# Seven block products for eight in the second output product of a two-layer gated network, with TensorE's order written out

## The chip, the cores and the metric

The program runs on one core of one Trainium2 chip. Its time is the device time of one execution, in microseconds (us). The kernel before takes 1388.17 us in the median of three runs (1387.19 to 1388.61).

## The reference

An attention with 32 memory slots for 8 batches of 8 heads (576 positions, head size 64) gives 4608 rows of 512. Two feed-forward blocks follow:

```python
def _moe_ref(x, w1, w2, w3, w_out) -> np.ndarray:      # d_ff 768
    h = np.maximum(np.maximum(x @ w1, x @ w2), x @ w3)
    return (h @ w_out).astype(np.float32)

def _moe2_ref(x, w_gate, w_val, w_out) -> np.ndarray:  # d_ff 1536
    gate = 1.0 / (1.0 + np.exp(-(x @ w_gate)))
    val = x @ w_val
    return (gate * val @ w_out).astype(np.float32)
```

All is float32. The change is in the last line, `gate * val @ w_out`: 4608 x 1536 by 1536 x 512.

## The kernel before

**Numbers.** An operand is split into a high part (a cast to a narrower float, by ScalarE: ACT) and the low rest (a subtraction, by GpSimd or VectorE: POOL or DVE); `w_split` does it. A product of two split operands is three matmuls, low by high, high by low, high by high (`PASSES`), added up in PSUM.

**Phase A** (to about 559 us) makes the attention and the first feed-forward block for pairs of batches, and writes its result to DRAM as `x2s`. While it ends, the first operands of phase B are loaded and split.

**Phase B** computes the second feed-forward block. The tokens are cut into five superchunks `sc` of 2 x 512, 2 x 512, 2 x 512, 2 x 384 and 2 x 384 tokens (`SUPER`, the 512 or 384 is `half`), the 1536 columns of gate and value into six pairs `j` of 128-wide slices (j and j + 6). One (sc, j) is called a chunk here; there are 18 with half 512 and 12 with half 384. In a chunk, x @ w is a 2 x 2 block product with seven products for eight (`ORDER` is 1, 6, 2, 7, 5, 4, 3), for gate (v = 0) and value (v = 1): `up(sc, j, pr, v)` is six matmuls of 128 x half. Sums between products are taken as PSUM is read. A finished block (c, h), c the half of the tokens and h the slice, goes through `block_done`: gate to a sigmoid, value times gate to a tile `gf`, and `gf` is split into `gg`. Block (0, 0) is finished by product 2, (1, 1) by 5, (1, 0) by 4 and (0, 1) by 3.

`down(sc, j, c, m)` multiplies 128 tokens of the two `gg` of half c by the two 128 x 512 slices of w_out: six matmuls of 128 x 512 into one PSUM bank `po` (two buffers), which are then copied (j = 0, ACT) or added (DVE, L777) to `acc`. A chunk has 8 (half 512) or 6 of them; they are traced between the `up` of the next chunk, and after j = 5 the rows are stored. The split parts of w_gate and w_val (`tb`) and of w_out (`wo`) are made in superchunk 0 (`t_make`, `wo_make`) and loaded from DRAM in the others (`t_load`, `wo_load`). The operand x of the next superchunk is loaded, summed and split (`x_load`, `x_sums`, `x_split`: tiles `xf`, `xa`) during the last chunks of the one before.

**What sets the order.** A scheduler lays the traced instructions out, engine by engine, in the order of its own timeline; each engine then works through its list in that order and waits on semaphores at the head of it. In phase B the scheduler sets TensorE's order as well.

Of the kernel before, what the change touches and what calls it, by code (L numbers as in the profile page):

```python
# [18 lines left out]
def attn_moe_kernel(  # L19
# [31 lines left out]

    def dma(o, i):
        ins = sync.dma_start(o, i)
# [334 lines left out]
    def x2_step(p, u, d):  # L388
        ps = bank()
        n = 0  # L390
        for j in range(J):
            for x, y in PASSES:
                pe.matmul(  # L393
                    ps[:, :U],
                    lhsT=wo1_t[:, x, (d * J + j) * 128:(d * J + j) * 128 + 128],
                    rhs=H[u, j][:, y],
                    start=(n == 0), stop=(n == 3 * J - 1),
                )
# [88 lines left out]
    def wo_load(sc, j):  # L487
        for h in range(2):
            t = WO[sc, j, h] = q4_tile("wo2")
            dma(f32(t), wos[j + h * NJ])  # L490
# [220 lines left out]

    def block_done(sc, j, v, c, h, ps, other):
# [18 lines left out]
        act.copy(t[:, 0, :half], gf)  # L731
        sub(pool, t[:, 1, :half], gf, f32(t[:, 0, :half]))

    def up(sc, j, pr, v):
# [12 lines left out]
        elif pr in (6, 7):  # L747
            u = E["u", pr, v] = small(f"u{pr}", 2)[:, :half]
            vec.tensor_tensor(out=u, in0=ps[:, :half], in1=E["p1", v], op=ALU.add)  # L749
# [9 lines left out]
    def down(sc, j, c, m):  # L759
        t0, half = SUPER[sc]  # L760
        ps = psB.tile([128, DM], F32, tag="po", name="po", bufs=2)
        n = 0
        for h in range(2):
            for x, y in PASSES:
                pe.matmul(  # L765
                    ps,
                    lhsT=GG[sc, j, c, h][:, x, 128 * m:128 * m + 128],
                    rhs=WO[sc, j, h][:, y],
                    start=(n == 0), stop=(n == 5),
                )  # L770
                n += 1
        if j == 0:
            t = ACC[sc, c, m] = b2.tile([128, DM], F32, tag="acc", name="acc", bufs=8)
            act.copy(t, ps)
        else:
            t = ACC[sc, c, m]
            vec.tensor_tensor(out=t, in0=ps, in1=t, op=ALU.add)  # L777
# [102 lines left out]
```

## Time and profile before

| what | us |
|---|---|
| median of three runs | 1388.17 |
| profiled execution: its time, its span | 1387.49, 1385.4 |
| busy in the span: TensorE matmul (PE) | 1337.5 |
| DVE, ACT, POOL | 863.1, 576.3, 514.6 |
| one chunk of half 512, of half 384, in the middle of a superchunk | 30.03, 22.70 |

A name such as `gg<-gf` is the tile written and the tiles read. PEld is the load of the stationary operand of a matmul, which overlaps the matmuls. L73 is the subtraction in a helper, whoever calls it.

### The profile page before, as it was taken

What the parts mean: (1) busy time and instruction counts of PE and PEld (TensorE: products, weight loads), DVE (VectorE), ACT (ScalarE), POOL (GpSimd) and SP (SyncE); (2) the same over time, 40 slices, a digit from 0 to 9 for tenths busy, and PEclk for the clock granted to TensorE, in tenths of its full rate; (3) what the DMA queues carried; (4) which work ended last, traced back from release to release, by engine and by line L of the source; (5) the groups of instructions that cost most, each with busy time, mean ns of one, the idle gap of its engine ahead of it and who ended that gap; (6) DMA issues with size and microseconds to landing.
All of it is one profiled execution on the core that took longest, in us unless ns stands there. A gap on an engine that the chain in (4) does not pass through costs nothing.

```text
span 1385.4 us, 22143 instructions
## 1 busy us (share of the span) xinstructions
PE 1337.5 (97%) x7864; PEld 1183.9 (85%) x7864; DVE 863.1 (62%) x1533; ACT 576.3 (42%) x1220; POOL 514.6 (37%) x454
## 2 busy tenths in 40 slices
PE   6688999999999999999999999999999999999998
PEld 3578899999999989788888888888888899999997
DVE  5999759966975895566765344453445444554454
ACT  5687546645654664453343321233222322233221
POOL 2775422422331227553586111461112712161111
PEclk9899999999999999999999999999999999999999
DMA  9588757776757745965556544465454666566651
GB/s 314 178 273 304 265 171 262 238 236 225 235 165 261 240 131 170 336 243 198 198 198 228 183 166 153 167 205 190 159 178 167 210 228 222 198 227 237 211 202 72
DMA packets 112269, 292.43 MB, mean 211 GB/s; under 512 B 12576, under 2 KB 28960, under 8 KB 112160
## 3 DMA queue, kind: packets, MB, share of 16 engines
q1 hardware_dynamic: 112160, 291.03, 61.9%
q8 instruction: 62, 1.02, 0.3%
q14 instruction: 47, 0.39, 0.1%
HBM read 224.92 MB, written 66.06 MB: 210 GB/s over the span
## 4 chain that ended last, share of the span: by engine, by line
PE 79%; DVE 10%; DMA 4%; issue 2%; ACT 2%; POOL 1%; SPq 1%; DVEq 0%; ACTq 0%; POOLq 0%
PE po L765 21%; PE px L698 15%; PE pv L698 10%; PE pz L698 10%; PE ps L393 9%; PE ps L370 8%; DVE g L73 2%; PE ps L343 2%; PE ps L209 1%; PE ps L246 1%; DVE ca L129 1%; DVE ca L128 1%; DMA raw<-wb_dram 1%; DVE hm L382 1%; DVE hm L381 1%
## 5 line engine op out<-in xcount | busy, mean ns | idle before, releaser
L765 PE MATMUL po<-wo,gg 128*128 128x512 f32 x1296 | 327.8, 392 | 1.0 <-POOL gg L73 1.0
L73 POOL TENSOR_TENSOR gg<-gf,gg 128x512 fp32r<-128x512 f32 (+1 forms) x120 | 143.4, 1195 | 469.1 <-ACT gg L731 426.3
L765 PEld LDWEIGHTS po<-wo,gg 128*128 128x128 f32 x1296 | 242.4, 188 | 49.5 <-POOL gg L73 1.3
L370 PE MATMUL ps<-attn,g 128*128 128x288 f32 x1728 | 258.7, 302 | 21.0 <-DVE g L73 11.0
L370 PEld LDWEIGHTS ps<-attn,g 128*128 128x128 f32 x1728 | 244.7, 193 | 31.8 <-DVE hm L381 8.7
L698 PE MATMUL px<-xa,tb 128*128 128x512 f32 (+1 forms) x1080 | 244.1, 368 | 1.6 <-DVE gf L729 1.1
L777 DVE TENSOR_TENSOR acc<-po,acc 128x512 f32<-128x512 f32 x180 | 124.3, 691 | 176.0 <-PE po L765 175.8
L698 PEld LDWEIGHTS px<-xa,tb 128*128 128x128 f32 x1080 | 198.0, 188 | 30.4 <-DVE gf L729 1.6
L698 PE MATMUL pz<-xa,tb 128*128 128x512 f32 (+1 forms) x720 | 169.5, 368 | 1.8 <-DVE u L749 1.8
L698 PE MATMUL pv<-xa,tb 128*128 128x512 f32 (+1 forms) x720 | 170.4, 369 | 0.0
L73 POOL TENSOR_TENSOR h<-hm,h 128x288 fp32r<-128x288 f32 x96 | 82.7, 864 | 211.8 <-DVE h L70 111.3
L393 PE MATMUL ps<-h,wo 128*128 128x288 f32 x1152 | 158.5, 296 | 0.0
L393 PEld LDWEIGHTS ps<-h,wo 128*128 128x128 f32 x1152 | 154.3, 188 | 2.8 <-issue 2.6
L698 PEld LDWEIGHTS pz<-xa,tb 128*128 128x128 f32 x720 | 132.2, 188 | 20.9 <-issue 2.2
L698 PEld LDWEIGHTS pv<-xa,tb 128*128 128x128 f32 x720 | 132.8, 189 | 18.1
L731 ACT CAST gg<-gf 128x512 fp32r<-128x512 f32 (+1 forms) x120 | 69.4, 578 | 176.3 <-DVE gf L727 130.5
L749 DVE TENSOR_TENSOR u<-pz,p 128x512 f32<-128x512 f32 (+1 forms) x120 | 76.2, 635 | 97.9 <-PE pz L698 93.4
L73 DVE TENSOR_TENSOR g<-ps,g 64x384 fp32r<-64x384 f32 x180 | 99.4, 552 | 31.8 <-ACT g L357 28.8
L721 ACT ACTIVATE sg<-sg 128x512 f32<-128x512 f32 (+1 forms) x90 | 53.1, 590 | 145.4 <-DVE sg L719 145.1
L357 ACT CAST g<-ps 64x384 fp32r<-64x384 f32 x192 | 90.7, 473 | 36.4 <-DVE g L73 22.4
L73 POOL TENSOR_TENSOR xa<-xf,xa 128x512 fp32r<-128x512 f32 (+1 forms) x64 | 78.8, 1252 | 21.6 <-ACT xa L134 21.6
L727 DVE TENSOR_TENSOR gf<-gf,sg 128x512 f32<-128x512 f32 (+1 forms) x90 | 70.9, 788 | 10.9 <-ACT sg L721 1.3
(92 smaller groups left out, 1394.4 us busy)
## 6 DMA issues: line engine op xcount, KB each, us to landing
tb<-tbs SPq DMA_DIRECT2D x168, 512.0 KB, 3.8
wx<-wxs SPq DMA_DIRECT2D x72, 384.0 KB, 3.9
wo<-wos SPq DMA_DIRECT2D x48, 512.0 KB, 5.4
tbs<-tb SPq DMA_DIRECT2D x42, 512.0 KB, 2.9
raw<-wb_dram SPq DMA_DIRECT2D x48, 384.0 KB, 3.5
kv<-kvm_dram SPq DMA_DIRECT2D x48, 256.0 KB, 5.3
raw<-wx_dram SPq DMA_DIRECT2D x24, 384.0 KB, 3.8
wxs<-wx SPq DMA_DIRECT2D x24, 384.0 KB, 4.4
```

The source lines that it names most:

```text
L73: eng.tensor_tensor(out=o, in0=a, in1=b, op=ALU.subtract)
L343: pe.matmul(ps[:, :384], lhsT=vt[:, x, 2 * e:2 * e + 2].rearrange("p a m -> p (a m)"), rhs=w[:, y], start=(n == 0), stop=(n == 2),)
L357: act.copy(t[r, 0], ps[r, :384])
L370: pe.matmul(ps[w][:, :U], lhsT=G[b, j, g][:, x, 128 * w:128 * w + 128], rhs=at[:, y, hf * U:hf * U + U], start=(n == 0), stop=(n == 5),)
L393: pe.matmul(ps[:, :U], lhsT=wo1_t[:, x, (d * J + j) * 128:(d * J + j) * 128 + 128], rhs=H[u, j][:, y], start=(n == 0), stop=(n == 3 * J - 1),)
L698: pe.matmul(ps[:, :half], lhsT=w[:, a, o:o + 128], rhs=x[:, k, c, :half], start=(first and n == 0), stop=(n == 5), skip_group_check=not first,
L721: act.activation(out=sg, in_=src, func=AF.Sigmoid)
L727: vec.tensor_tensor(out=gf, in0=gf, in1=sg, op=ALU.mult)
L731: act.copy(t[:, 0, :half], gf)
L749: vec.tensor_tensor(out=u, in0=ps[:, :half], in1=E["p1", v], op=ALU.add)
L765: pe.matmul(ps, lhsT=GG[sc, j, c, h][:, x, 128 * m:128 * m + 128], rhs=WO[sc, j, h][:, y], start=(n == 0), stop=(n == 5),)
L777: vec.tensor_tensor(out=t, in0=ps, in1=t, op=ALU.add)
```

## The change

The product gg @ w_out of a chunk becomes a 2 x 2 block product as well, with seven products for eight: rows are the two halves c of the tokens, the inner dimension the two slices h, columns the two halves of the 512 outputs (`HD` = 256).

- `down(sc, j, pr, q)` does up to two groups of 128 tokens of product pr, three matmuls of 128 x 256 each, into one `po` bank: 14 of them in a chunk (7 products in the order `DORDER` = 1, 6, 7, 5, 4, 2, 3, two q each; with half 384 the second has one group). One follows each of the 14 `up` of the next chunk.
- `block_done` makes the sums of `gf`: after block (1, 0) three (L772 and two subtractions), after (0, 1) one, on POOL, in the last chunk on DVE. Seven `gg` are split in a chunk, before four. The left factors are 1: block (0, 0); 4: (1, 1); 6, 7 and 5: the sums made when (1, 0) is there; 2: (0, 1); 3: the sum made when (0, 1) is there.
- The seven products are summed over j in seven `acc` tiles (128 x 4 x 256). Only in the downs of j = 5, which run in the first chunk of the next superchunk, are they added to each other (`BEFORE`, `add`, L811: four adds on POOL, three on DVE, each of 1024 elements a partition, 768 with half 384; in the last superchunk all seven on DVE).
- `wo` becomes seven tiles of 128 x 2 x 256 a chunk, made or loaded one by one in `down`.
- In phase B TensorE's instructions are kept in the order in which the code is written (`InOrder`).
- Buffers: 8 `q4` for 11, 7 `acc` of 4 KB a partition for 8 of 2 KB, 8 `gg` for 6; `tw` has two buffers in another pool, so the load for j = 1 waits for the last use of j = 0; u7 takes p1's place. `x_split` alternates POOL and DVE; `x_sums` is traced in chunk j = 4 from superchunk 1 on.

```diff
     queue = {"in order": True, "last weights": None}
+    class InOrder:
+        def __getattr__(self, name):
+            fn = getattr(self.eng, name)
+            return lambda *a, **k: tc.keep_in_program_order(fn(*a, **k))
...
-    NQ = 11
+    NQ = 8
     ORDER = (1, 6, 2, 7, 5, 4, 3)
+    DORDER = (1, 6, 7, 5, 4, 2, 3)
+    HD = DM // 2
...
         for h, i in enumerate((j, j + NJ)):
-            t = TW[j, h] = tile()
+            t = TW[j, h] = b1.tile([128, 2, DM], F32, tag="tw", name="tw", bufs=2)
             dma(t.rearrange("p h c -> p (h c)"), wbf[i, :, 0:2 * DM])
...
-    def wo_make(j):
-        for h, i in enumerate((j, j + NJ)):
-            WO[0, j, h] = kept(TW[j, 2][:, h], wos[i], "wo2", vec if h else pool)
+    def wo_make(j, pr):
...
+        WO[0, j, pr] = kept(wo_tile(), src, wos[j, pr - 1], vec if pr in (5, 2) else pool)
...
+    pe = InOrder(nc.tensor)
...
+    def gg_split(sc, j, pr, x):
+        half = SUPER[sc][1]
+        t = GG[sc, j, pr] = b2.tile([128, 2, 512], F32R, tag="gg", name="gg", bufs=8)
+        w_split(x, t[:, 0, :half], t[:, 1, :half])
...
-        t = GG[sc, j, c, h] = b2.tile([128, 2, 512], F32R, tag="gg", name="gg", bufs=6)
-        act.copy(t[:, 0, :half], gf)
-        sub(pool, t[:, 1, :half], gf, f32(t[:, 0, :half]))
+        if (c, h) == (0, 0):
+            gg_split(sc, j, 1, gf)
+        elif (c, h) == (1, 1):
+            gg_split(sc, j, 4, gf)
+        elif (c, h) == (1, 0):
+            A11, A22 = F[0, 0], F[1, 1]
+            eng = vec if (sc, j) == LAST else pool
+            eng.tensor_tensor(out=A22, in0=gf, in1=A22, op=ALU.add)
+            sub(eng, gf, A11, gf)
+            sub(eng, A11, A22, A11)
+            for pr, x in ((6, A11), (7, gf), (5, A22)):
+                gg_split(sc, j, pr, x)
+        else:
+            gg_split(sc, j, 2, gf)
+            sub(vec if (sc, j) == LAST else pool, gf, gf, F[0, 0])
+            gg_split(sc, j, 3, gf)
...
+    def add(sc, x, y):
+        n = SUPER[sc][1] // 128
+        a, b = ACC[sc, x][:, :n], ACC[sc, y][:, :n]
+        (vec if x in (3, 5) or sc == LAST[0] else pool).tensor_tensor(out=a, in0=a, in1=b, op=ALU.add)
...
+    BEFORE = {1: ((2, 1),), 7: ((7, 6), (4, 7)), 6: ((6, 1),), 5: ((3, 5), (3, 6), (5, 7))}
+    def down(sc, j, pr, q):
+        n = SUPER[sc][1] // 128
+        m0, m1 = 2 * q, min(2 * q + 2, n)
...
+        for m in range(m0, m1):
+            for n, (x, y) in enumerate(PASSES):
                 pe.matmul(
-                    ps,
-                    lhsT=GG[sc, j, c, h][:, x, 128 * m:128 * m + 128],
-                    rhs=WO[sc, j, h][:, y],
-                    start=(n == 0), stop=(n == 5),
+                    ps[:, m - m0],
+                    lhsT=GG[sc, j, pr][:, x, 128 * m:128 * m + 128],
+                    rhs=WO[sc, j, pr][:, y],
+                    start=(n == 0), stop=(n == 2),
                 )
...
+        if j == NJ - 1:
+            for x, y in BEFORE.get(pr, ()):
+                add(sc, x, y)
...
                 for v in range(2):
                     up(sc, j, pr, v)
-                    slot += 1
-                    if slot >= 3 and downs:
+                    if downs:
                         down(*downs.pop(0))
...
-            downs = [(sc, j, c, m) for c in (1, 0) for m in range(SUPER[sc][1] // 128)]
+            downs = [(sc, j, pr, q) for pr in DORDER for q in range(2)]
```

**Place 1, from superchunk 1 to 2.** POOL in the change, after block (1, 0) of chunk (1, 5) is finished (`gf_11420` is block (1, 1), `gf_11468` block (1, 0), `gf_11334` block (0, 0); `gg_11474`, `gg_11477` and `gg_11480` are the left factors of products 6, 7 and 5; `acc_10251` and `acc_10053` are the sums of products 2 and 1; `xf_12994` is a sum of x for superchunk 3):

```order
L772 TENSOR_TENSOR gf_11420<-gf_11468,gf_11420 128x512
L82 TENSOR_TENSOR gf_11468<-gf_11334,gf_11468 128x512
L82 TENSOR_TENSOR xa_11545<-xf_11078,xa_11545 128x512
L82 TENSOR_TENSOR xa_11545<-xf_11178,xa_11545 128x512
L82 TENSOR_TENSOR gf_11334<-gf_11420,gf_11334 128x512
L537 TENSOR_TENSOR xf_12994<-xf_12739,xf_12741 128x384
L811 TENSOR_TENSOR acc_10251<-acc_10251,acc_10053 128x1024
L82 TENSOR_TENSOR gg_11474<-gf_11334,gg_11474 128x512
L82 TENSOR_TENSOR xf_12996<-xf_12994,xf_12737 128x384
L82 TENSOR_TENSOR xf_12739<-xf_12737,xf_12739 128x384
L82 TENSOR_TENSOR gg_11477<-gf_11468,gg_11477 128x512
L82 TENSOR_TENSOR gg_11480<-gf_11420,gg_11480 128x512
```

POOL before, at the same place (`gg_10634` and `gg_10662` are the last two of the four blocks):

```order
L73 TENSOR_TENSOR xa_10639<-xf_10179,xa_10639 128x512
L73 TENSOR_TENSOR xa_10639<-xf_10187,xa_10639 128x512
L73 TENSOR_TENSOR gg_10634<-gf_10631,gg_10634 128x512
L73 TENSOR_TENSOR xa_10667<-xf_10433,xa_10667 128x512
L73 TENSOR_TENSOR xa_10667<-xf_10438,xa_10667 128x512
L73 TENSOR_TENSOR gg_10662<-gf_10659,gg_10662 128x512
```

TensorE in the change, the first instructions of chunk (2, 0) (`gg_11336` is the left factor of product 1; the first `up` of the chunk is the first row):

```order
L59 MATMUL px_11552<-xa_11264,tb_11262 128x512 x6
L59 MATMUL po_11561<-wo2_11260,gg_11336 128x256 x6
L59 MATMUL px_11569<-xa_11264,tb_11262 128x512 x6
L59 MATMUL po_11578<-wo2_11260,gg_11336 128x256 x6
L59 MATMUL pz_11591<-xa_11307,tb_11305 128x512 x6
L59 MATMUL po_11600<-wo2_11303,gg_11474 128x256 x6
L59 MATMUL pz_11608<-xa_11307,tb_11305 128x512 x6
```

An add of two `acc`, whose second operand is complete only when the second row of product 1 (`po_11578`) has been added to `acc_10053`, now stands on POOL ahead of the split of `gg_11474`, which is the sixth of these TensorE rows.

The same place from superchunk 0 to 1, POOL in the change, from the first of the three sums after block (1, 0) of chunk (0, 5) to the split for product 6 (`gg_9652`; `wo2_9721` belongs to the split of w_out, `acc_8257` and `acc_8028` are the sums of products 2 and 1):

```order
L772 TENSOR_TENSOR gf_9595<-gf_9646,gf_9595 128x512
L82 TENSOR_TENSOR xa_9727<-xf_9421,xa_9727 128x512
L82 TENSOR_TENSOR xa_9727<-xf_9426,xa_9727 128x512
L82 TENSOR_TENSOR wo2_9721<-wv_9376,wo2_9721 128x256
L82 TENSOR_TENSOR gf_9646<-gf_9504,gf_9646 128x512
L537 TENSOR_TENSOR xf_11176<-xf_10921,xf_10923 128x512
L811 TENSOR_TENSOR acc_8257<-acc_8257,acc_8028 128x1024
L82 TENSOR_TENSOR gf_9504<-gf_9595,gf_9504 128x512
L82 TENSOR_TENSOR xf_11178<-xf_11176,xf_10919 128x512
L82 TENSOR_TENSOR xf_10921<-xf_10919,xf_10921 128x512
L82 TENSOR_TENSOR gg_9652<-gf_9504,gg_9652 128x512
```

Here six instructions of other work stand among the three sums and the split: two of `xa`, one of `wo2`, three of `xf`, besides the add of two `acc`.

**Place 2, the start of phase B.** ACT before, then in the change (`tb_7812` before, and `tb_7805`, `tb_7835` and `tb_7865` in the change, are products 1, 6 and 2 of j = 1; `p1` is the copy of the first product out of PSUM):

```order
L68 COPY x2_7724<-ps_7705 128x288
L68 COPY x2_7746<-ps_7727 128x288
L68 COPY x2_7776<-ps_7757 128x288
L746 COPY p1_7801<-px_7794 128x512
L746 COPY p1_7810<-px_7803 128x512
L134 CAST tb_7812<-tw_7787 128x512
```

```order
L143 CAST tb_7805<-tw_7780 128x512
L77 COPY x2_7768<-ps_7749 128x288
L143 CAST tb_7835<-td_7833 128x512
L143 CAST tb_7865<-tw_7780 128x512
L794 COPY p1_7794<-px_7787 128x512
L794 COPY p1_7803<-px_7796 128x512
```

The two copies `p1` moved from ahead of the first cast for j = 1 to behind three of them.

**Place 3, the end.** DVE in the change, in the last superchunk (`acc_15613`, `acc_15564`, `acc_15523` and `acc_15488` are the sums of products 3, 2, 4 and 5; the last rows before the end):

```order
L811 TENSOR_TENSOR acc_15523<-acc_15523,acc_15452 128x768
L844 TENSOR_TENSOR acc_15564<-px_16773,acc_15564 128x512
L811 TENSOR_TENSOR acc_15613<-acc_15613,acc_15488 128x768
L844 TENSOR_TENSOR acc_15564<-px_16782,acc_15564 128x256
L844 TENSOR_TENSOR acc_15523<-po_16758,acc_15523 128x512
L844 TENSOR_TENSOR acc_15523<-po_16767,acc_15523 128x256
L811 TENSOR_TENSOR acc_15613<-acc_15613,acc_15417 128x768
L811 TENSOR_TENSOR acc_15488<-acc_15488,acc_15452 128x768
L844 TENSOR_TENSOR acc_15613<-pz_16788,acc_15613 128x512
L844 TENSOR_TENSOR acc_15613<-pz_16797,acc_15613 128x256
```

Before, six adds `acc<-po,acc` 128x512 (L777) alone end DVE's list; now there are 14 of L844 and seven of L811 behind the last `up`.

More of the change, by code (lines that the diff above doesn't have):

```diff
@@ L485, in t_load, with wo_load @@
         dma(f32(t), tbs[j, pr - 1])
[L487 to L490, printed above, removed]
+    def wo_load(sc, j, pr):
+        t = WO[sc, j, pr] = wo_tile()
+        dma(f32(t), wos[j, pr - 1])
     XA = {}
@@ L678, in attn_moe_kernel @@
                 fn(*a)
+    xo.release()
     low.release()
@@ L747, in up @@
         elif pr in (6, 7):
-            u = E["u", pr, v] = small(f"u{pr}", 2)[:, :half]
-            vec.tensor_tensor(out=u, in0=ps[:, :half], in1=E["p1", v], op=ALU.add)
+            p1 = E["p1", v]
+            u = E["u", pr, v] = p1 if pr == 7 else small("u6", 2)[:, :half]
+            vec.tensor_tensor(out=u, in0=ps[:, :half], in1=p1, op=ALU.add)
         elif pr == 2:
@@ L757, in up @@
             block_done(sc, j, v, 0, 1, ps, E["u", 6, v])
-    def down(sc, j, c, m):
-        t0, half = SUPER[sc]
[L761 to L764, printed above, removed]
+    def add(sc, x, y):
+        n = SUPER[sc][1] // 128
+        a, b = ACC[sc, x][:, :n], ACC[sc, y][:, :n]
+        (vec if x in (3, 5) or sc == LAST[0] else pool).tensor_tensor(out=a, in0=a, in1=b, op=ALU.add)
+    BLOCK = {2: (0, 0), 3: (0, 1), 4: (1, 0), 5: (1, 1)}
@@ new lines, in store @@
+    def store(sc, pr, m0, m1):
+        t0, half = SUPER[sc]
+        c, d = BLOCK[pr]
+        r0 = t0 + c * half
+        dma(out[r0 + 128 * m0:r0 + 128 * m1, d * HD:d * HD + HD].rearrange("(m p) d -> p m d", p=128),
+            ACC[sc, pr][:, m0:m1])
+    BEFORE = {1: ((2, 1),), 7: ((7, 6), (4, 7)), 6: ((6, 1),), 5: ((3, 5), (3, 6), (5, 7))}
+    def down(sc, j, pr, q):
+        n = SUPER[sc][1] // 128
+        m0, m1 = 2 * q, min(2 * q + 2, n)
+        tag = "po" if (sc, j) != LAST else ("po", "px", "pz", "pv")[(2 * DORDER.index(pr) + q) // 2 % 4]
+        ps = psB.tile([128, 512], F32, tag=tag, name=tag, bufs=2).rearrange("p (m d) -> p m d", m=2)
+        for m in range(m0, m1):
+            for n, (x, y) in enumerate(PASSES):
@@ L774, in down @@
-            act.copy(t, ps)
-        else:
-            t = ACC[sc, c, m]
-            vec.tensor_tensor(out=t, in0=ps, in1=t, op=ALU.add)
-        if j == NJ - 1:
-            r0 = t0 + c * half + m * 128
-            dma(out[r0:r0 + 128, :], t)
+            if q == 0:
+                ACC[sc, pr] = b2.tile([128, 4, HD], F32, tag="acc", name="acc", bufs=7)
+            act.copy(ACC[sc, pr][:, m0:m1], ps[:, :m1 - m0])
+        else:
+            t = ACC[sc, pr][:, m0:m1]
+            vec.tensor_tensor(out=t, in0=ps[:, :m1 - m0], in1=t, op=ALU.add)
@@ L782, in attn_moe_kernel @@
+        if j == NJ - 1 and pr in (2, 3, 4):
+            store(sc, pr, m0, m1)
+        if q == 0:
+            return
+        if j == NJ - 1:
+            for x, y in BEFORE.get(pr, ()):
+                add(sc, x, y)
+            if pr == 5:
+                store(sc, 5, 0, SUPER[sc][1] // 128)
+        if (sc, j) != LAST:
+            nxt = after(sc, j)
+            if nxt[0] == 0:
+                wo_make(nxt[1], pr)
+            else:
+                wo_load(*nxt, pr)
     tw_load(1)
+    wv_load(0)
```

62 lines of the change are left out of this document (37 added, 25 removed).

## Prediction

> **What bounds the kernel now.** I began with the page's shares of the engines, then cut phase B into chunks with the view of busy time by stretch, then asked who TensorE waits for, and read the price of a matmul from the chain of work that ended last.
>
> ```profile
> PE 1337.5 (97%) x7864; PEld 1183.9 (85%) x7864; DVE 863.1 (62%) x1533; ACT 576.3 (42%) x1220; POOL 514.6 (37%) x454
> ```
>
> ```profile
> core 0: us, PE busy (x) PEld busy (x) DVE busy (x) ACT busy (x) POOL busy (x), PEclk, DMA share, GB/s
> ...
> 644.31:674.34 30.03, 30.03 (x133) 24.78 (x133) 21.45 (x29) 10.37 (x19) 11.11 (x10) 1.00 0.57 209
> ...
> 794.44:824.47 30.03, 30.03 (x134) 24.78 (x133) 14.74 (x22) 6.04 (x11) 5.19 (x4) 1.00 0.45 158
> ...
> 1281.65:1304.35 22.70, 22.70 (x120) 21.19 (x120) 12.18 (x22) 4.92 (x10) 3.94 (x4) 1.00 0.62 201
> ```
>
> ```profile
> PE pz L698 <- DVE u L749: 1.8, 1, 1.8
> PE po L765 <- POOL gg L73: 1.0, 1, 1.0
> ```
>
> ```profile
> 185.10 11.90 PE ps L393 x90
> ...
> 794.44 2.72 PE px L698 x12
> ...
> 1100.28 2.75 PE po L765 x12
> ...
> 1144.37 2.08 PE px L698 x12
> ```
>
> In the stretches (start:end, length, then busy time of each engine) TensorE is busy for the whole of each chunk, and in all of phase B it waits some microseconds. The chunk is the sum of its matmuls: 84 x 0.2267 + 48 x 0.2292 = 30.04 us, with 2.72 / 12 and 2.75 / 12 us a matmul, and the row says 30.03. So every matmul saved is worth its price, and every wait that TensorE gets costs its length. The other engines have room in the mean: POOL 5.2 of 30 us. Whether they have it at each moment is what the change asks, since TensorE can no longer be given other work.
>
> **TensorE's saving.** A chunk has 84 matmuls of 128x256 in `down` for 48 of 128x512 (half 384: 63 for 36). The trace has none of 256 columns. By columns the price runs 0.1322 us (11.90 / 90, 288 columns), 0.1733 (384), 0.2267 (512): about 0.42 ns a column, which gives 0.120 at 256, and 0.121 if `down` stays 1% dearer, as at 512. It can't be above the 0.1322 of 288 columns; a floor from loading a new stationary operand is bounded by transposes with 128 moving columns:
>
> ```profile
> 400.86 0.60 PE L195 MATMUL ps<-ident,et 128*128 128x128 f32 x4
> ...
> L195 PE MATMUL ps<-ident,et x64: 270/272/477, 8.4 to 401.2; 128*128 128x128 f32 x64
> ```
>
> Four take 0.60 us and one alone 0.27, so (0.60 - 0.27) / 3 = 0.11 us apart. I take 0.121. Half 512: 11.00 - 84 x 0.121 = 0.84 us, 18 times 15.1; half 384: 8.25 - 63 x 0.121 = 0.63, 12 times 7.5. **-22.6 us** (-24.9 at 0.120; +2.8 at 0.1322).
>
> [...]
>
> **The handovers between superchunks.** Prices on POOL and DVE (groups by shape, then instructions in order of time):
>
> ```profile
> L73 POOL TENSOR_TENSOR gg<-gf,gg 128x512 fp32r<-128x512 f32 x72 | 94.7, 1315 | 267.8 <-ACT gg L731 224.9 <-PE po L765 40.9 <-DMA tw<-wbf 1.9
> ...
> L73 POOL TENSOR_TENSOR gg<-gf,gg 128x384 fp32r<-128x384 f32 x48 | 48.7, 1015 | 201.4 <-ACT gg L731 201.4
> ...
> L777 DVE TENSOR_TENSOR acc<-po,acc 128x512 f32<-128x512 f32 x180 | 124.3, 691 | 176.0 <-PE po L765 175.8
> ```
>
> ```profile
> 540.44 2.54 POOL L73 TENSOR_TENSOR xa<-xf,xa 128x512 fp32r<-128x512 f32 x2
> ...
> 545.88 3.43 POOL L73 TENSOR_TENSOR xa<-xf,xa 128x512 fp32r<-128x512 f32 x2
> ```
>
> ```profile
> 549.77 1.78 DVE L73 TENSOR_TENSOR td<-tw 128x512 f32<-128x512 f32 x1
> ...
> 573.65 0.69 DVE L73 TENSOR_TENSOR td<-tw,td 128x512 f32<-128x512 f32 x1
> 574.26 0.69 DVE L73 TENSOR_TENSOR td<-tw 128x512 f32<-128x512 f32 x1
> ```
>
> POOL starts such instructions 1.25 us apart at 512 columns, 0.95 at 384; when DVE also reads two SBUF tiles, both slow, to 1.7 and 1.78. The slope (1.315 - 1.015) / 128 = 2.3 ns a column makes an add of 1024 columns 2.4 us, of 768 1.85 (estimates from these rows). DVE starts 0.61 apart.
>
> The front's place 1 shows the trap. POOL's add of `acc` stands ahead of the split for product 6 and waits until the last row of product 1 is added on DVE. TensorE does one `up` meanwhile and then wants that split. Wait: DVE add + POOL add + split - `up`, whatever came earlier. From superchunk 1 to 2: 0.69 + 2.4 + 1.25 - 1.36 = 3.0; from 2 to 3, where `up` has 384 columns, 3.3; from 3 to 4, with 768, 0.45 + 1.85 + 0.95 - 1.04 = 2.2. From 0 to 1 the list is longer: nine instructions at 1.25, one of 256 at 0.65 and the add are 14.3, begun when block (1, 0) is done on DVE, 2.3 to 4 us after its `up`; TensorE wants the split after 5 `down` and 5 `up`, 5 x 0.73 + 5 x 1.36 = 10.4. Wait 6.2 to 7.9; I take 7.5. Sum **16.0**.
>
> Behind them DVE stands at the add for product 4 until POOL's add of sums 7 into 4, eleven POOL instructions after the split: 2 x 0.95 + 6 x 1.25 + 3 x 2.4 = 16.6, with the DVE add 17.3; queued behind are the reads that free `po`. TensorE has 8 `up` and 8 `down` until it needs that bank: 16.7 (half 512) or 14.2 (from 2 to 3): waits of 0.6 and 3.1; nothing at the others, whose lists are shorter. **3.7.** The slowing of both engines isn't in these: some three POOL instructions at +0.45 and three adds of DVE at up to twice their price for each handover, 0 to 3 us; I take 1.5 each, **6**. Handovers together **25.7** (15 to 36). In the middle of a superchunk there is slack: POOL has the sums (three at 1.25) and the split done about 9 us after block (1, 0)'s `up`, and it is wanted at 10.4, so these cost nothing; without that cover each chunk would pay what is late.
>
> **The clock after a wait.**
>
> ```profile
> 573.00:580.00 7.00, 3.61 (x14) 2.41 (x15) 6.90 (x9) 3.53 (x7) 4.84 (x3) 1.00 0.58 219
> 580.00:584.00 4.00, 4.00 (x13) 3.12 (x12) 3.79 (x7) 2.88 (x5) 3.34 (x4) 0.60 0.97 311
> ```
>
> After 3.4 us idle in 7 the granted clock is 0.60 for 4 us, a loss of 1.6. One such loss from 0 to 1, and half of one from 2 to 3: **2.5** (0 to 6.4). [...]
>
> **The end.**
>
> ```profile
> 1369.89 2.24 PE L698 MATMUL pv<-xa,tb 128*128 128x384 f32 x12
> ...
> 1373.13 8.53 PE L765 MATMUL po<-wo,gg 128*128 128x512 f32 x36 [1.00 <-POOL gg L73]
> ...
> 1381.69 0.69 DVE L777 TENSOR_TENSOR acc<-po,acc 128x512 f32<-128x512 f32 x1 [0.68 <-PE po L765]
> ```
>
> Before, the last `up` ends at 1372.13 and the span 13.3 us later, 8.25 of it `down`, 5.0 not. After it, DVE now has four operations on `gf` and `acc` (1.8), then seven times 0.61 + 0.34 + 0.88 (512, 256 and 768 columns), 12.8, from 1.1 on, some 1 in waits, and 3.0 for the last store as now: 19.7, of which 8.0 are `down`. 11.7 for 5.0: **+6.5** (4 to 9).
>
> **The start.**
>
> ```profile
> 560.74 0.59 ACT L746 COPY p<-px 128x512 f32<-128x512 f32 x1 [0.36 <-PE px L698]
> ...
> 570.78 0.62 ACT L134 CAST tb<-tw 128x512 fp32r<-128x512 f32 x1 [8.08 <-DMA tw<-wbf]
> ```
>
> ```profile
> 573.46 1.63 PE L698 MATMUL px<-xa,tb 128*128 128x512 f32 x6 [0.50 <-ACT sg L721]
> 576.21 1.65 PE L698 MATMUL px<-xa,tb 128*128 128x512 f32 x6 [1.12 <-DVE gf L729]
> 579.67 2.35 PE L698 MATMUL pz<-xa,tb 128*128 128x512 f32 x7 [1.81 <-DVE u L749]
> ```
>
> ```profile
> 558.66 1.30 POOL L73 TENSOR_TENSOR tb<-tw,tb 128x512 fp32r<-128x512 f32 x1
> ...
> 565.79 0.53 SPq L53 DMA_DIRECT2D tw<-wbf  x1
> ```
>
> ACT waits for the load of `tw` for j = 1, and TensorE idles 3.4 us later. In the change the `p1` copies stand behind that cast, and product 2, which adds into the same bank, behind them. The load may start once POOL's last use of the old `tw` (559.96) is over, near 561.5, and lands 5 us later; two DVE steps, two casts and a copy make 570. TensorE finishes product 6 at 564.6: idle 5.4 for 3.4, **+2** (-2 to +6, as SP's queue of stores lets the load pass).
>
> **Superchunk 0.** Chunks in which weights are split have DVE at 21.45 us; six more `acc` adds (+3.7), one 512-wide subtraction less (-1.2) and six of 256 (+2.7) make 26.7 of 29.2, and POOL goes from 11.1 to 22. Both are dense, and POOL's splits for `tb` stand among the sums: **+2** (0 to 8). Transfers: 0.8 MB more a chunk at a share of 0.45 to 0.57 hide.
>
> **Sum.** -22.6 + 25.7 + 2.5 + 6.5 + 2 + 2 = +16.1 on the profiled 1387.49: 1403.6, and the median lies 0.7 above that execution, so 1404.
>
> **Rivals.** (1) *POOL's list hardly holds.* Only the forced waits occur (6.2 + 3.0 + 3.3 + 2.2 = 14.7), the end costs 4.5, a matmul 0.120: -24.9 + 14.7 + 4.5 = -5.7, 1382. For it: POOL idles two thirds of the middle chunks; against: its list is fixed. It decides where handovers and end together cost less than 23. Chance 0.14. (2) *Loading weights sets the pace* at 256 columns, 0.132: +41, 1429. PEld busy at 97% of the 288-column stretch speaks for it, the transposes at 0.11 against. 0.08. (3) *DVE becomes the bound* in superchunk 0 and in chunks with `xa` and `acc` adds, 10 us for 2: 1412. 0.13. (4) *The change does not pay and does not cost*: handovers 10 us cheaper and no loss of clock, 1389 to 1391. 0.09. My forecast: 0.56, its own range 1392 to 1416.
>
> A measurement of this kernel tells about 0.2% (2.8 us) from no change. Faster by more: case 1, 0.14. Within: case 4, 0.09. Slower: 0.77. The range of 1386 to 1424 leaves out most of cases 1 and 2.
>
> **What will show it.** The groups by shape: `down` 12 in 1.45 us. The waits of TensorE: `po` on POOL's `gg`, four times, 2 to 9 us, in the first chunk of superchunks 1 to 4, and `po` on DVE's `acc` from 2 to 3. Middle chunks at 29.2 and 22.2 us. DVE as the last engine for some 8 us after the last matmul. If TensorE shows no waits of over a microsecond at the handovers, or middle chunks stay at 30, I am wrong.

## The result, and the profile after

The changed kernel takes 1454.1 us in the median of four runs (1453.16 to 1456.16); the kernel before, on the same chip, 1387.7. The ratio is 1.0486, 95% interval 1.0463 to 1.0508: slower, by four times what was forecast (1404). The profiled execution took 1453.16 us, with a span of 1451.4, 66.0 longer than before.

First the page's shares of the engines after, for the rows of before in the prediction:

```profile
PE 1339.4 (92%) x8836; PEld 1225.5 (84%) x8836; DVE 1042.6 (72%) x1780; ACT 636.9 (44%) x1374; POOL 799.3 (55%) x676
```

TensorE is as long busy as before (1337.5), though it has fewer columns to multiply, and the program is 66 us longer. That each chunk did become shorter shows in TensorE's rows, in order of time, in the middle of a superchunk. Each pair of rows is the same `up` of two chunks that follow each other:

```profile
830.27 1.55 PE L59 MATMUL px<-xa,tb 128*128 128x512 f32 x6
...
859.43 1.55 PE L59 MATMUL px<-xa,tb 128*128 128x512 f32 x6
...
1206.18 1.21 PE L59 MATMUL px<-xa,tb 128*128 128x384 f32 x6
...
1228.20 1.21 PE L59 MATMUL px<-xa,tb 128*128 128x384 f32 x6
```

A chunk takes 29.16 us for 30.03, and 22.02 for 22.70. The matmul of 256 columns costs what was hoped: (29.16 - 84 x 0.2267) / 84 = 0.120 us. Over phase B that is 18 x 0.87 + 12 x 0.68 = 23.8 us saved. The waits ate it. The view of TensorE's waits has, of phase B (line, what it waits for: us in all, times, longest):

```profile
PE po L59 <- POOL gg L82: 32.3, 9, 8.7
PE po L59 <- DVE acc L844: 11.7, 8, 2.0
...
PE px L59 <- ACT p L794: 9.0, 1, 9.0
PE po L59 <- issue: 7.3, 2, 4.4
```

In order of time they are 9.0 at the start, 19.1 inside superchunk 0 and up to the first product of the next, 34.0 at the four handovers and 2.3 at the end: 64.4 us for 4.4. The one at the start, and the larger ones of superchunk 0 and the first handover:

```profile
571.34 4.59 PE L59 MATMUL px<-xa,tb 128*128 128x512 f32 x12 [8.99 <-ACT p L794]
596.12 1.65 PE L59 MATMUL po<-wo,gg 128*128 128x256 f32 x6 [3.76 <-POOL gg L82]
...
707.90 1.65 PE L59 MATMUL po<-wo,gg 128*128 128x256 f32 x6 [1.98 <-DVE acc L844]
...
732.60 1.65 PE L59 MATMUL po<-wo,gg 128*128 128x256 f32 x6 [4.04 <-POOL gg L82]
...
777.48 1.65 PE L59 MATMUL po<-wo,gg 128*128 128x256 f32 x6 [8.75 <-POOL gg L82]
778.93 2.76 PE L59 MATMUL pz<-xa,tb 128*128 128x512 f32 x6
781.49 1.48 PE L59 MATMUL po<-wo,gg 128*128 128x256 f32 x6
```

Six matmuls of 256 columns take 0.87 in such a row where no wait precedes them, and 1.65 here: the clock, granted at 0.50 in those rows. The view by stretch gives it behind two waits (the first is one of 2.00 us, which ends at 641.83), and for chunks 1 to 5 of superchunk 0 how full the engines are (columns as in the prediction):

```profile
588.03:765.08 177.05, 157.98 (x848) 135.68 (x846) 148.87 (x187) 82.12 (x158) 154.11 (x119) 0.94 0.59 207
...
641.83:648.00 6.17, 6.17 (x27) 5.39 (x28) 5.04 (x10) 1.70 (x5) 1.33 (x2) 0.72 0.55 212
...
777.48:782.70 5.22, 5.22 (x18) 4.64 (x19) 1.38 (x2) 0.17 (x1) 4.94 (x4) 0.50 0.02 2
```

POOL is busy 154 of 177 us, 87%, and DVE 84%. The same view of the kernel before has, for five of its chunks there, 60% and 66%:

```profile
590.00:740.00 150.00, 150.00 (x661) 123.81 (x660) 98.54 (x131) 62.68 (x108) 89.68 (x68) 1.00 0.59 213
```

**The ledger.** Matmuls at full clock would fill 18 x 29.16 + 12 x 22.02 = 789.1 us of phase B, before 812.9. TensorE was busy 821.1 in it, before 818.1; that is 32.0 above full clock, before 5.1. Most of this extra is the clock: in phase B the trace has thirteen stretches with a granted clock of 0.50, 71.7 us in all, in which TensorE is busy 53.8. Half of that, 26.9, is the loss; before it is 1.7, in one stretch. The rest, 5.1 for 3.4, is not followed up here; a part of it is that the first matmuls after a wait take longer at full clock too (in the last section's row at 1300.06 six take 0.98 us for 0.87). After the last matmul 9.1 us follow for 3.7, and phase B begins 2.4 earlier. The span moves by -23.8 (matmuls) + 60.0 (waits) + 25.2 (clock) + 1.7 (that rest) + 5.3 (after the last matmul) - 2.4 = 66.0.

### The profile page after: what moved, and what is told of

It is laid out like the page before. It is cut to its first block, busy times and chain, and to the rows that moved or that the text cites. A ratio compares the mean times of both kernels' runs of the same rounds, so it can differ in the third digit from the quotient of the medians.

```text
span 1451.4 us, 25227 instructions
## 1 busy us (share of the span) xinstructions
PE 1339.4 (92%) x8836; PEld 1225.5 (84%) x8836; DVE 1042.6 (72%) x1780; ACT 636.9 (44%) x1374; POOL 799.3 (55%) x676
## 4 chain that ended last, share of the span: by engine, by line
PE 63%; DVE 13%; POOL 10%; issue 6%; DMA 5%; ACT 2%; SPq 0%; DVEq 0%; POOLq 0%; ACTq 0%
PE po L59 15%; PE px L59 12%; PE pz L59 9%; PE ps L379 8%; PE ps L402 8%; PE pv L59 7%; POOL gg L82 3%; PE ps L352 2%; DVE g L82 2%; POOL gf L82 1%; DVE ca L138 1%; DVE ca L137 1%; PE ps L218 1%; POOL xa L82 1%; POOL xf L82 1%
## 5 line engine op out<-in xcount | busy, mean ns | idle before, releaser
L59 PEld LDWEIGHTS po<-wo,gg 128*128 128x128 f32 x2223 | 325.8, 195 | 80.9 <-POOL gg L82 36.0
L59 PE MATMUL po<-wo,gg 128*128 128x256 f32 x2223 | 341.1, 288 | 53.4 <-POOL gg L82 32.3
L82 POOL TENSOR_TENSOR gg<-gf,gg 128x512 fp32r<-128x512 f32 (+1 forms) x210 | 254.1, 1228 | 216.4 <-ACT gg L143 215.9
L844 DVE TENSOR_TENSOR acc<-po,acc 128x512 f32<-128x512 f32 x340 | 215.7, 635 | 87.3 <-PE po L59 85.0
L59 PE MATMUL px<-xa,tb 128*128 128x512 f32 (+1 forms) x1080 | 258.8, 376 | 9.0 <-ACT p L794 9.0
L59 PEld LDWEIGHTS px<-xa,tb 128*128 128x128 f32 x1080 | 191.8, 193 | 28.9 <-ACT p L794 9.4
L143 ACT CAST gg<-gf 128x512 fp32r<-128x512 f32 (+1 forms) x210 | 111.9, 576 | 145.0 <-POOL gf L82 64.9
L59 PEld LDWEIGHTS pv<-xa,tb 128*128 128x128 f32 x720 | 126.3, 191 | 12.8
L82 POOL TENSOR_TENSOR gf<-gf 128x512 f32<-128x512 f32 (+1 forms) x87 | 105.9, 1218 | 5.3
L366 ACT CAST g<-ps 64x384 fp32r<-64x384 f32 x192 | 90.5, 473 | 37.1 <-DVE g L82 21.4
L762 DVE TENSOR_TENSOR gf<-gf,sg 128x512 f32<-128x512 f32 (+1 forms) x90 | 81.4, 905 | 2.1 <-ACT sg L756 0.2
L798 DVE TENSOR_TENSOR u<-pz,p 128x512 f32<-128x512 f32 (+1 forms) x60 | 38.1, 636 | 53.9 <-PE pz L59 51.2
```

Of the source, the lines that this page charges most:

```text
L59: return lambda *a, **k: tc.keep_in_program_order(fn(*a, **k))
L82: eng.tensor_tensor(out=o, in0=a, in1=b, op=ALU.subtract)
L143: act.copy(hi, w)
L366: act.copy(t[r, 0], ps[r, :384])
L762: vec.tensor_tensor(out=gf, in0=gf, in1=sg, op=ALU.mult)
L798: vec.tensor_tensor(out=u, in0=ps[:, :half], in1=p1, op=ALU.add)
```

## The experiments

Two theories stood after this. The *order* theory is the prediction's: POOL and DVE stand at additions that wait for each other. The *throughput* theory: where weights are split, and where operands for the next superchunk are, POOL and DVE are too full to deliver in time, whatever their order. A time is compared with the kernel before on the same chip: 1381.5 for the first four runs (one time each), 1384.7 for the next three, 1385.1 for the last two. The change and the two rows "both" are medians of four executions, the others are one each; the kernel before spread over 4 to 6 us in seven executions on one chip, so differences of that size between rows show nothing.

| run | us over before | waits in phase B: start, superchunk 0, handovers, end | extra busy time, of it clock |
|---|---|---|---|
| the change | 66.4 | 9.0, 19.1, 34.0, 2.3 | 32.0, 26.9 |
| no additions | 36.4 | 6.7, 20.1, 16.4, 1.9 | 19.1, 13.1 |
| no sums | 33.9 | 8.4, 7.8, 22.7, 0 | 16.9, 12.7 |
| POOL in written order | 102 | 7.9, 28.9, 54.9, 1.9 | 31.1, 24.7 |
| TensorE free | 72.2 | 55.3 in all | 37.1, 14.8 |
| additions on DVE | 50.5 | 8.6, 19.0, 23.3, 2.5 | 24.1, 17.9 |
| product 4 second | 46.2 | 8.2, 16.9, 19.0, 2.7 | 27.2, 19.2 |
| both, and more | 33.7 | 6.6, 20.3, 14.1, 5.3 | 18.4, 10.2 |
| no splits of w_out | 22.6 | 5.6, 12.6, 11.3, 5.3 | 18.1, 11.7 |
| both, order of the start | 32.8 | 5.5, 18.5, 12.7, 5.3 | 20.4, 12.6 |

"Extra busy time" is TensorE's busy time in phase B less 789.1; "of it clock" is half of its busy time in the stretches in which the granted clock is 0.50. The waits of a place are added up from TensorE's rows in order of time, as above. The border between superchunk 0 and the first handover is drawn by time, near 766 us (760 in the run without splits of w_out, which is ahead), so a wait of some microseconds can stand on either side of it.

**The additions of `acc` left out.**

```diff
-    BEFORE = {1: ((2, 1),), 7: ((7, 6), (4, 7)), 6: ((6, 1),), 5: ((3, 5), (3, 6), (5, 7))}
+    BEFORE = {}
```

> The seven additions of acc tiles to each other (L811) at the end of each superchunk are left out, so the output is not the reference's; all else stays. In the changed kernel TensorE waits 34 us at the four handovers (0 to 1: 8.75 and 1.80; 1 to 2: 1.94, 3.92, 2.88; 2 to 3: 5.62, 4.44; 3 to 4: 3.17, 1.52) and 19 us inside superchunk 0. Order theory (the prediction's: POOL and DVE stand at additions that wait): the first waits of the handovers all but vanish, 34 falls under 8, with the clock some 1415 us. Throughput theory (POOL is simply full there, it stands at nothing): the first waits fall only by the 2.35 us that one addition takes on POOL, 23.4 to about 14, the second ones (DVE behind its three additions) go; about 1426 us. Both: superchunk 0 keeps its 19 us.

TensorE's rows at the handovers without them:

```profile
774.13 1.65 PE L59 MATMUL po<-wo,gg 128*128 128x256 f32 x6 [6.50 <-POOL gg L82]
...
950.00 0.95 PE L59 MATMUL po<-wo,gg 128*128 128x256 f32 x6 [1.93 <-POOL gf L772]
957.60 0.98 PE L59 MATMUL po<-wo,gg 128*128 128x256 f32 x6 [3.19 <-POOL gg L82]
1135.57 0.98 PE L59 MATMUL po<-wo,gg 128*128 128x256 f32 x6 [3.33 <-POOL gg L82]
1273.13 0.97 PE L59 MATMUL po<-wo,gg 128*128 128x256 f32 x6 [1.42 <-POOL gg L82]
```

The first waits fall from 23.4 to 16.4, by 1.75 each, less than one addition takes, and do not vanish. The second ones go. The time, 36.4 above before, is near what the throughput theory gave (1426 where before is 1388, +38; the order theory +27). So POOL did not stand at an addition in the first waits. The changed kernel's own POOL rows at the handover from 0 to 1 say the same. A wait would stand in brackets; there is none before 783.78:

```profile
767.74 1.28 POOL L82 TENSOR_TENSOR gf<-gf 128x512 f32<-128x512 f32 x1
768.98 1.26 POOL L537 TENSOR_TENSOR xf<-xf 128x512 f32<-128x512 f32 x1
770.20 2.34 POOL L811 TENSOR_TENSOR acc<-acc 128x1024 f32<-128x1024 f32 x1
772.50 1.26 POOL L82 TENSOR_TENSOR gf<-gf 128x512 f32<-128x512 f32 x1
773.72 2.49 POOL L82 TENSOR_TENSOR xf<-xf 128x512 f32<-128x512 f32 x2
776.17 4.97 POOL L82 TENSOR_TENSOR gg<-gf,gg 128x512 fp32r<-128x512 f32 x4
```

When POOL came to the addition at 770.20, DVE had finished its row for 2.1 us. At the other three handovers POOL has no wait in front of its first addition either. The list was as the prediction read it; POOL was later than it assumed.

**The sums of `gf` left out.** The splits work on the blocks themselves.

```diff
-            eng = vec if (sc, j) == LAST else pool
-            eng.tensor_tensor(out=A22, in0=gf, in1=A22, op=ALU.add)
-            sub(eng, gf, A11, gf)
-            sub(eng, A11, A22, A11)
...
-            sub(vec if (sc, j) == LAST else pool, gf, gf, F[0, 0])
```

> The four POOL instructions a chunk that make the sums of gf (three after block (1, 0), one after (0, 1)) are left out, the splits then work on the blocks themselves: the output is not the reference's, POOL has 5 to 6 us less in each chunk. Throughput theory: POOL is busy 28 to 33 of 34 us in the chunks of superchunk 0; the 19 us of waits there fall under 6, and what they cost in clock goes with them, 1420 to 1430 us. Prediction's theory (slack of a microsecond or two, superchunk 0 costs 2 us): waits in superchunk 0 change by less than 4 us, 1447 to 1454.

Inside superchunk 0 every wait on `gg` is gone. What is left there, 7.8 us, waits for DVE. The time, 33.9 above before, is what the throughput theory asked for (1420 to 1430 for 1388, +32 to +42); the waits stay a little above its 6 us. At the handovers the first waits go too, and the second ones grow: TensorE comes earlier to the place where DVE holds it. This run takes POOL's time away and three steps between a block and its splits with it, so it can't tell a full engine from a long chain; the run without splits of w_out, below, can. DVE's rows at the first handover:

```profile
764.02 3.80 DVE L806 TENSOR_TENSOR acc<-acc 128x1024 f32<-128x1024 f32 x1
...
768.34 1.21 DVE L806 TENSOR_TENSOR acc<-acc 128x1024 f32<-128x1024 f32 x1
...
776.13 1.29 DVE L839 TENSOR_TENSOR acc<-po,acc 128x512 f32<-128x512 f32 x2 [3.45 <-POOL acc L806]
```

This is the prediction's second hold, DVE at product 4's row until POOL has added sums 7 into 4. The same addition takes 1.21 us on DVE alone and 3.80 beside one of POOL.

**POOL's instructions in the written order.**

```diff
     pe = InOrder(nc.tensor)
+    pool = InOrder(nc.gpsimd)
```

> POOL's instructions of phase B keep the order in which the code is written: the split for product 6 stands ahead of the addition of acc and ahead of the splits of weights that the scheduler had put before it. No work is removed. Order theory: the waits of TensorE on POOL's gg (32 us in all) fall under 10 us and the time to 1410 to 1425. Throughput theory: at the handover from 0 to 1 and in superchunk 0 POOL is full whatever the order, so half of the waits or more stay or turn up elsewhere (weights split too late), 1435 to 1460.

At the handovers from 1 to 2 and 3 to 4 the waits on POOL fall to about a microsecond, because the split for product 6 now stands ahead of the addition. But then POOL reaches its additions late, and DVE, whose own list still has them early, stands behind them:

```profile
1003.12 2.27 DVE L812 TENSOR_TENSOR acc<-acc 128x1024 f32<-128x1024 f32 x1 [1.64 <-POOL acc L59]
1007.62 1.23 DVE L812 TENSOR_TENSOR acc<-acc 128x1024 f32<-128x1024 f32 x1 [2.23 <-POOL acc L59]
1011.08 1.29 DVE L845 TENSOR_TENSOR acc<-po,acc 128x512 f32<-128x512 f32 x2 [2.23 <-POOL acc L59]
```

TensorE waits 9 to 12 us at each handover for the reads behind them. In superchunk 0 the waits grow to 28.9. Both expected times missed, though waits did turn up elsewhere, as the throughput theory said: I had ordered one of two engines that wait for each other. So the order does matter at the handovers, and it does not help superchunk 0.

**TensorE's order left to the scheduler.**

```diff
-    pe = InOrder(nc.tensor)
```

> TensorE's instructions of phase B are no longer kept in the written order, as before the change. Theory that the fixed order turns each late split into a wait: the 64 us of waits in phase B fall by a half or more, and the clock loss with them, 1405 to 1425 us. Theory that POOL's pace bounds superchunk 0 and the handovers: TensorE runs out of other work as soon as two PSUM banks are taken, the waits fall by less than 15 us, 1435 to 1455.

Waits fall by 9 us only, and the time does not fall, as the theory of POOL's pace expected. The scheduler puts the `down` together, and then two banks don't carry them. The stationary loads of three groups of 12, where nothing but `down` runs:

```profile
1107.14 1.49 PEld L831 LDWEIGHTS po<-wo,gg 128*128 128x128 f32 x12 [1.54 <-DVE acc L843]
1108.91 1.50 PEld L831 LDWEIGHTS po<-wo,gg 128*128 128x128 f32 x12 [0.28 <-DVE acc L843]
1110.67 1.52 PEld L831 LDWEIGHTS po<-wo,gg 128*128 128x128 f32 x12 [0.26 <-DVE acc L843]
```

They start 1.77 us apart for 12 x 0.120 = 1.44. The fixed order, with an `up` between, avoids that: in a middle chunk of the change TensorE is busy 29.16 of 29.16 us. Setting it free does not help; whether another order of TensorE would is not shown.

**All additions on DVE; product 4 second.** Two single edits.

```diff
-        (vec if x in (3, 5) or sc == LAST[0] else pool).tensor_tensor(out=a, in0=a, in1=b, op=ALU.add)
+        vec.tensor_tensor(out=a, in0=a, in1=b, op=ALU.add)
```

> All seven additions of acc tiles at a superchunk's end are on DVE, which also adds the rows into these tiles; nothing crosses from one engine to the other there, and POOL has 9.6 us less at each handover. Theory that DVE's list stands behind additions that wait for POOL (in the run with POOL in written order those waits were 9 to 12 us at each handover): the second waits at the four handovers (1.80, 2.88, 4.44, 1.52) go, the first ones fall by 2.35 each as without additions; 1420 to 1430 us by the clock of this chip 1388 for the kernel before, superchunk 0 keeps 19 us. Theory that DVE's own work is what is late at the handovers: with four more additions of 1.2 to 2.4 us on it the second waits grow, 1450 or more.

```diff
-    DORDER = (1, 6, 7, 5, 4, 2, 3)
+    DORDER = (1, 4, 6, 7, 5, 2, 3)
+    WORDER = (1, 6, 4, 7, 5, 2, 3)
...
-        if j == NJ - 1 and pr in (2, 3, 4):
+        if j == NJ - 1 and pr in (2, 3):
...
+            if pr == 7:
+                store(sc, 4, 0, SUPER[sc][1] // 128)
...
-            if nxt[0] == 0:
-                wo_make(nxt[1], pr)
-            else:
-                wo_load(*nxt, pr)
+            for p in {4: (), 6: (6, 4)}.get(pr, (pr,)):
+                if nxt[0] == 0:
+                    wo_make(nxt[1], p)
+                else:
+                    wo_load(*nxt, p)
...
-                    wo_make(0, DORDER[ORDER.index(pr)])
+                    wo_make(0, WORDER[ORDER.index(pr)])
```

> The order in which the products of gg @ w_out follow is 1, 4, 6, 7, 5, 2, 3 for 1, 6, 7, 5, 4, 2, 3, so the first product that needs a sum of gf is wanted by TensorE two up and two down later, 4.2 us. No work is removed. Theory that superchunk 0's waits are lateness of the sums and their splits on POOL (3.76, 0.88, 0.87, 1.30, 4.04 us): these go, as do the first ones at the handovers, 1425 to 1435 us. Theory that POOL is full in superchunk 0 over the whole chunk: the waits come back at a later product or on DVE, and the time stays above 1440.

The additions on DVE take 16 us off. The second waits shrink from 10.6 to 3.2 in all, so DVE's own work was not too much; additions on two engines at once were. The gain is short of what was expected (+50 for +32 to +42): the first waits fell by 3.3 in all, not by 2.35 each. Product 4 second takes 20 off. The waits on `gg` inside superchunk 0 do go, as the first theory says, and the time, 1431, is in its range too. But 16.9 us of waits stay there, 13.5 of them on DVE now, as the second says: with four microseconds more for the sums, the next engine is late. Most of the gain is at the handovers.

**Both edits,** with three more: in the last superchunk three additions on POOL; ScalarE's copies of product 1 ahead of the cast that waits for a load; the parts of w_out that DVE's sums wait for made by DVE. (The cast of the weights for j = 1 is held in the same way as the copies; those lines are left out.)

```diff
+        (pool if sc == LAST[0] and x in (2, 6, 7) else vec).tensor_tensor(out=a, in0=a, in1=b, op=ALU.add)
...
-        WO[0, j, pr] = kept(wo_tile(), src, wos[j, pr - 1], vec if pr in (5, 2) else pool)
+        WO[0, j, pr] = kept(wo_tile(), src, wos[j, pr - 1], vec if pr in (1, 6) else pool)
...
-            act.copy(p1, ps[:, :half])
+            ins = act.copy(p1, ps[:, :half])
+            if (sc, j) == (0, 0):
+                tc.keep_in_program_order(ins)
```

> Both edits together (additions on DVE, in the last superchunk three of them on POOL; product 4 second), and besides the copies of the first product on ScalarE stand ahead of the cast that waits for its load, and DVE makes the split parts of w_out that its own sums wait for. If order and engines of these few instructions are the whole cause, TensorE's waits in phase B fall from 64 to under 15 us and the clock loss from 26 to under 8: 1375 to 1390 us, the kernel before at 1388. If the pace of POOL and DVE in superchunk 0 is a cause of its own, 10 to 15 us of waits and 10 of clock stay there: 1395 to 1410.

1418.4 us, ratio 1.0246 to the kernel before (1.0229 to 1.0263). Both expected times are missed (1375 to 1390, 1395 to 1410). The handovers are down to 14.1. Superchunk 0 keeps 20.3, more than even the second theory left there. The view by stretch shows how full the engines are: in 30 us of it DVE is busy 28.6 and POOL 29.2.

```profile
690.00:720.00 30.00, 26.64 (x142) 22.48 (x141) 28.57 (x36) 12.23 (x24) 29.16 (x22) 0.94 0.46 176
```

**Less work in superchunk 0.** As the last run, with two changes at the start: DVE's differences of weights for j = 1 and its additions to the first chunk's `u` keep the written order, and w_out for j = 0 is split by the engines that the change has. Once with the loads, sums and splits of w_out for j = 1 to 5 left out, once complete. (The line that takes out the loads isn't shown.)

```diff
-                    wo_make(nxt[1], p)
+                    WO[0, nxt[1], p] = WO[0, 0, p]
+                    dma(wos[nxt[1], p - 1], f32(WO[0, 0, p]))
```

> As the run with both edits together, with DVE's additions for the second product also ahead of the differences of weights that wait for the second load, and in superchunk 0 the parts of w_out are summed and split for j = 0 only and used and stored again for the other j: the sums and splits of w_out for j = 1 to 5 are left out, and the output is not the reference's. That is about 4 us of POOL and 5 us of DVE a chunk less; sums and splits of gf stay. Theory that POOL's and DVE's pace over the whole chunk is the limit in superchunk 0 (POOL 29 us busy of 30, DVE 28.6 there): TensorE's waits inside superchunk 0, 20 us in the run with both edits, fall under 6, the time to 1385 to 1395. Theory that the limit is the chain from a block's end over sums and split to TensorE, which holds nothing of w_out: they stay above 14, 1405 to 1415. The start: 6.6 us of waits fall to 3 to 4 if the order on DVE was what was late.

> The same without leaving anything out: all edits that keep the output (product 4 second, additions on DVE and in the last superchunk three on POOL, order of the start on ScalarE and DVE, DVE's choice among the parts of w_out). Against the run with both edits only the start moves, 2.5 to 4 us of waits and up to 2 of clock: 1413 to 1417 where the kernel before has 1385. Throughput theory for superchunk 0: its 20 us of waits stay.

The same stretch of superchunk 0 in both runs, first without and then with the splits of w_out:

```profile
631.00:750.00 119.00, 114.99 (x651) 99.76 (x650) 101.67 (x133) 45.54 (x80) 96.67 (x69) 0.99 0.50 185
```

```profile
631.00:750.00 119.00, 104.67 (x571) 88.84 (x570) 110.28 (x142) 51.54 (x99) 107.79 (x82) 0.97 0.60 214
```

With POOL at 81% for 91 and DVE at 85% for 93 the waits inside superchunk 0 are 12.6 us for 18.5, and 8.6 of the 12.6 are one wait that the complete run does not have. The three waits on POOL's `gg` (2.88, 2.68 and 3.37) are gone, and of 9.6 us on DVE's `acc` 4.0 are left. The chain from a block over its sums and splits is the same in both, so it is the engines' pace that limits. (ScalarE and the transfers have less to do as well; no wait of TensorE in superchunk 0 names either in the complete run.) The time, 1407.7, missed the 1385 to 1395 of this theory and lies in the range of the other, whose waits above 14 us are not there. The wait of 8.60 stands behind DVE, which makes the differences of the weights for j = 2 at 619.51, after two rows of `acc`; in the complete run it does so at 608.08. Product 6 needs their splits. First the run without splits of w_out, then the complete one:

```profile
618.90 0.69 DVE L854 TENSOR_TENSOR acc<-po,acc 128x512 f32<-128x512 f32 x1 [1.41 <-PE po L59]
619.51 1.16 DVE L465 TENSOR_TENSOR td<-tw 128x512 f32<-128x512 f32 x1
```

```profile
608.08 1.78 DVE L465 TENSOR_TENSOR td<-tw 128x512 f32<-128x512 f32 x1 [0.90 <-DMA tw<-wbf]
```

Without that wait and the 3 us of clock behind it this run would take some 1396 us (an estimate from its rows). The complete run takes 1417.9, ratio 1.024 (1.0222 to 1.0258), the same as the one before it and above the 1413 to 1417 expected: the start's waits fell from 6.6 to 5.5, not to 3 or 4, since another step of DVE was late next. No version beat the kernel before. Eight products in superchunk 0 alone, or parts of w_out made in phase A, were not tried.

## Why the prediction was wrong

The direction was right and the size wrong, 66.4 us for 16. By its terms:

| term | predicted | measured |
|---|---|---|
| TensorE's saving | -22.6 | -23.8 |
| handovers, waits | 25.7 | 34.0 |
| superchunk 0 | 2 | 19.1 |
| start | 2 | 5.6 |
| end | 6.5 | 6.6 (1.3 of waits, 5.3 after the last matmul) |
| the clock after waits | 2.5 | 25.2 |
| the rest of TensorE's extra busy time | 0 | 1.7 |
| start of phase B | 0 | -2.4 |

**TensorE's saving** and **the end** were right. 256 columns cost 0.120 us, not the 0.132 of the rival in which loading weights sets the pace; that rival falls. After the last matmul DVE works off rows and additions, as was forecast. (The prediction's own figures for the end, 11.7 for 5.0, give 6.7; it wrote 6.5.)

**Superchunk 0** is the step that failed. It took the engines' busy time over the chunk, 26.7 us of DVE and 22 of POOL in 29.2, and put 2 us on that. POOL's 22 was 1.25 us an instruction; in the trace POOL is busy 24 to 28 in each 30 us, and a split of `gg` takes it 1.45 there (28 in 40.6). More than the mean, the work comes in bursts: after block (1, 0) three sums and three splits at once, behind parts of weights that were put between them. The prediction had found slack of a microsecond and a half for this in the middle of a superchunk, which holds there: in four superchunks no middle chunk waits. Where weights are split it called both engines dense, but put 2 us (0 to 8) on that without working out when the splits are there and when they are wanted. The runs without sums and without splits of w_out show that it was the load. Rival 3 named the place (DVE, 10 us for 2, chance 0.13), with half its price and one of its two engines.

**The clock** is the term that was mis-sized most, 25.2 for 2.5. One loss and a half were counted; there are thirteen stretches at half clock. The size was read from one loss after 3.4 us of idle time in 7; here a wait of 2.00 starts a loss (0.72 over the next 6.2 us), and the last section sets it beside a longer wait that starts none. Over the runs with TensorE in order the clock costs 0.2 to 0.4 us for each microsecond of waits, 0.42 in the change. The terms for waits had to be multiplied by about 1.4.

**The handovers** came out near the forecast sum for another reason. The order that the prediction read is there, yet POOL stands at nothing in the first waits; it is late with its whole list, of which an addition is one item of 2.35 us. The run without additions shows that. The second hold was sized at 3.7 and is 10.6 (1.80, 2.88, 4.44, 1.52): DVE adds three times while POOL adds too. That the two engines do wait for each other there shows in the runs without sums and with POOL in order, and the additions on DVE alone remove it.

**The start** was right in its mechanism: the copies stand on ScalarE behind a cast, and that behind DVE, which waits for the load. The wait is 8.99 for 5.4 for two reasons. Phase B began 2.4 us earlier, so TensorE was through with product 6 at 562.4, not 564.6; that part is paid back in the last row of the table. And the load, put at 561.5 and 5 us, went out at 561.1 and took 6.9, so DVE and ScalarE were later:

```profile
569.66 0.62 ACT L143 CAST tb<-td 128x512 fp32r<-128x512 f32 x1 [6.89 <-issue]
...
570.71 1.06 ACT L794 COPY p<-px 128x512 f32<-128x512 f32 x2
```

## What to carry to other kernels

When products are cut to save matmuls, the sums and splits land on the engines that feed TensorE; add up each of those engines for the fullest stage, not for the mean one, with the durations that they have beside each other. If TensorE's time is the program's time, a wait costs its length and can cost clock on top, 0.2 to 0.4 of its length on the mean here, so the 24 us saved here are gone with some nine waits of 2 us. Work that two engines hand back and forth in a fixed list belongs on one of them, as moving the additions to DVE did.

## What the runs showed of the hardware

- The length of a wait alone did not say what it cost in clock. In the traces of before and of the change the granted clock is 1.00 or 0.50, and it stays at one of them for 3.41 us or a whole multiple of that (the last time alone is cut off by the end). Of the thirteen times at 0.50 in phase B of the change seven last 3.41 us, four 6.83 and two 10.24. The wait of 2.00 us lies within one stretch of 3.41 us (busy 1.41), and the next one runs at 0.50:

```profile
639.60:643.01 3.41, 1.41 (x10) 1.14 (x9) 3.41 (x6) 1.71 (x4) 3.36 (x4) 1.00 0.83 328
643.02:646.43 3.41, 3.41 (x13) 2.91 (x12) 3.05 (x7) 0.53 (x2) 0.18 (x1) 0.50 0.27 104
646.43:649.84 3.41, 3.41 (x19) 2.91 (x19) 2.62 (x4) 1.36 (x3) 1.28 (x2) 1.00 0.44 172
```

  The longer wait of 3.17 us falls into two stretches, 1.49 in one and 1.68 in the other, and the clock stays at 1.00. The next `up` after its row takes 1.21 us as anywhere:

```profile
1294.97:1298.38 3.41, 1.92 (x12) 1.60 (x11) 1.19 (x3) 2.23 (x5) 3.41 (x4) 1.00 0.80 266
1298.38:1301.79 3.41, 1.73 (x12) 1.73 (x13) 0.69 (x1) 0.00 (x0) 3.41 (x4) 1.00 0.17 64
1301.79:1305.21 3.42, 3.42 (x25) 3.42 (x24) 1.58 (x3) 0.91 (x2) 3.34 (x4) 1.00 0.60 193
```

```profile
1300.06 0.98 PE L59 MATMUL po<-wo,gg 128*128 128x256 f32 x6 [3.17 <-POOL gg L82]
1300.88 1.21 PE L59 MATMUL pz<-xa,tb 128*128 128x384 f32 x6
```

  Counted over phase B of these two traces, a stretch at 1.00 was followed by one at 0.50 in none of 460 cases with up to 1.68 us idle, in 3 of 4 with 1.77 to 1.81, and in all 11 with 1.94 or more. A stretch at 0.50 was followed by one at 1.00 in all 14 cases with up to 0.47 us idle and by another at 0.50 in all 8 with 0.83 or more. So in these two traces the price of a wait depended on where it fell among the stretches.
- DVE and POOL slowed each other at the additions more than the prediction took (0.45 us an instruction on POOL, up to twice the price on DVE). An addition of 1024 elements takes 1.21 us on DVE with POOL idle and 3.80 beside POOL's in the run without sums (768.34 and 764.02), and 3.04 beside POOL's in the change (792.16). POOL's takes 2.39 beside that one and 3.38 and 3.33 beside others of DVE (981.33, 1168.20), for 2.34 to 2.41 with none beside it.
